# Load order and opening of a fused S5 scan and GEGLU kernel: one queue for nearly all loads, the D row spread by a product, dt computed as a row, sines ahead of the first Gelu

## The chip, the cores and the metric

The kernel runs on one core of one Trainium2 chip. The time is the device time of one execution in microseconds; the kernel before has a median of 190.36 us over three runs (189.83 to 191.79).

## The reference, cut to what matters

```python
xn = _layernorm(x)                        # x: [1, 2048, 512] bf16
# A: a diagonal complex recurrence over 2048 steps, state width P = 512
dt = jnp.exp(log_dt); Lam_bar = jnp.exp(dt * Lam)
B_bar = ((Lam_bar - 1.0) / Lam)[:, None] * Bmat
Bu = jnp.einsum("bld,pd->blp", xn + 0j, B_bar)
h = Lam_bar[None, :] * h + Bu[:, t, :]    # for t in range(L)
s = 2.0 * jnp.einsum("blp,dp->bld", hseq, Cmat).real + xn * Dskip
# B: GEGLU feed-forward, F = 1376
g = silu((gelu(xn @ w_gate) * (xn @ w_up)) @ w_down)
out = x + s * g
```

The weights w_gate and w_up are [512, 1376], w_down is [1376, 512], B and C have a real and an imaginary part of [512, 512] each. log_dt, Lambda_re, Lambda_im and Dskip are vectors of 512. Everything comes in bf16.

## The kernel before, in words

The 2048 tokens are cut into four chunks of 512 (index s), and each chunk into four tiles of 128 tokens (index m). For each chunk the kernel does five things.

- It normalises the tiles (`stats`, `rstd`, `norm_dve`; for chunks 2 and 3 `norm_act`, on ScalarE, whose sums go through the tile `junk`) and transposes them to `xnT`: chunk 0 on TensorE (`head_t`, four 128x128 transposes and an eviction by ScalarE, L341), the later chunks by DMA transposes (`dma_t`, L363).
- It multiplies `xnT` by w_gate and w_up. F is cut into thirds of 512, 512 and 352 columns. The products go into one of three PSUM slots of two banks; ScalarE evicts them to `gt` (with the Gelu) and `ub`, VectorE multiplies both to `at`, and a DMA transpose brings `at` to `atT` (L454). In chunk 0 the three thirds are done one after the other for all four tiles (`first_chunk`, then `gate_pair`, L385 to L391); in later chunks tile by tile (`gate_tile`).
- `half(s, h)` computes one half of the 512 complex states: products of `BT` and `xnT` (L530), evicted by ScalarE to `U` (L533), a rotation of `U` by tables of sines and cosines (L544, L552), a real scan with the decay `rho` (L563), and the rotation back into `hst`. This turns the complex recurrence into two real ones.
- `down_pair` multiplies `atT` by w_down and puts a Silu on it (`g2`).
- `y_tile` multiplies `hst` by the scaled C (`C2`), adds the skip term `sk` = xn times the D row, multiplies by `g2`, adds x and stores the tile.

Before that, small parameters are prepared. The three vectors log_dt, Lambda_im and Lambda_re come into a tile `pv` of 12 rows and are turned into columns by one transpose on TensorE and a copy `pf` (L622, L623). GpSimd raises e to log_dt (`dt_`) and, after VectorE's multiplication, e to dt times Lambda_re (`rho`); both are `power`, at L320. VectorE makes an angle `ang` and a folded angle `kr` for 49 table entries (L589 to L593), ScalarE takes their sines and cosines (L594, L595) and VectorE builds the full tables `tab` from them by six products and sums (L609). ScalarE's Gelu, Silu and sine lie in tables of which one is loaded at a time; a change of table is an ACT_TABLE_LOAD.

The columns of C are scaled by coefficients (`coefficients`, L672 to L690) that need `rho` and the sines; C itself comes by two DMA transposes into the second `hst` buffer (`CT`, L739). For each of four blocks ScalarE makes a product `tF` (L742) and VectorE two more (L744, L747).

The order of the work is made by a planner (`Plan`). Each step is added with its engine, a cost, a lag until others see its result, what it reads and writes, and a rank. TensorE's steps keep the order in which they are added; the steps of the other engines are put in order by a list scheduler that tries priorities with random changes and keeps the best. The costs and lags are written out by hand. Instructions of one engine run in the planned order, and an instruction that waits holds up everything behind it on that engine. DMAs issued by SP, ACT and POOL are rows of those engines' streams.

The loads of the kernel before: x tiles 0 and 2, the first two thirds of w_gate, the second chunk of x and both parts of B go through SP; x tiles 1 and 3 and the first two thirds of w_up through ACT; `pv`, the D row (copied to all 128 partitions by the DMA, L649), the last thirds of w_gate and w_up and w_down (L652, L653) through POOL. Ten matmuls on a zeroed tile `warm` (L330) fill TensorE's time until the first tile is normalised.

Of the kernel before, what the change touches and what calls it, by code (L numbers as in the profile page):

```python
# [18 lines left out]
LOOK, HOLD, TABLE, ROUNDS, TRIALS = 0.3, 8.0, 6.0, 6, 600  # L19
# [3 lines left out]
class Plan:  # L23
# [89 lines left out]
    def run(self):  # L113
# [38 lines left out]
def kernel(  # L152
# [55 lines left out]
    pv = sb("pv", [12, P])  # L208
# [25 lines left out]
    def small(name, w=NPT):  # L234
        return sb(name, [P, w], FP32)
# [30 lines left out]
    def load_w(put, eng, q, c, land, which, **kw):  # L266
        a, b = CH[c]
        nm, w, r = (("wg", wg, wg_r), ("wu", wu, wu_r))[which]
        put(eng, 0.47, land, lambda w=w, r=r: q.dma_start(out=w[:, :, a:b], in_=r[:, :, a:b]), writes=[(nm, c)], **kw)
# [5 lines left out]
    dma_first(SP, 0.5, 8.5, lambda: nc.sync.dma_start(out=x_tok[:, M : 2 * M, :], in_=x_r[:, M : 2 * M, :]), [("x", 1, m) for m in range(M)])  # L275
    for i, v in enumerate((A_log_dt, A_Lambda_im, A_Lambda_re)):
        dma(POOL, 0.6, 4.3, lambda i=i, v=v: G.dma_start(out=pv[4 * i : 4 * i + 4, :], in_=v.rearrange("(k p) -> k p", p=P)),
            writes=[("pv", i)], rank=200.0)
    ident = sb("ident", [P, P])
    pool(0.8, lambda: make_identity(nc, ident[:]), writes=["ident"], rank=190.0)  # L280

    warm = sb("warm", [P, TS])
# [5 lines left out]
    dve(480, lambda: V.memset(warm[:], 0.0), writes=["warm"], not_before=0.6, rank=300.0)  # L288
# [6 lines left out]
    acts(1, lambda: act(out=tiny[:], in_=zero[:], func=AF.Silu), ["zero"], ["tiny"], table="silu", rank=150.0)  # L295
# [17 lines left out]
    def stats(s, m):  # L313
        def f():
            V.bn_stats(out=st[:, s, m, :], in_=x_tok[:, s * M + m, :])
        dve(512, f, [("x", s, m)], [("st", s, m)])
        dve(6, lambda: V.bn_aggr(out=mv[:, s, m, :], in_=st[:, s, m, :]), [("st", s, m)], [("mv", s, m)])
# [489 lines left out]
```

## Time and profile before

| | |
|---|---|
| median of three runs | 190.36 us |
| the profiled execution | 189.71 us |
| its span, first to last instruction | 187.9 us |
| mean granted TensorE clock | 0.982 |
| TensorE, VectorE, ScalarE, GpSimd busy | 176.6, 159.2, 117.3, 15.4 us |
| first gate product | at 8.93 us |
| last product ends | at about 183.8 us |
| HBM read and written | 6.46 MB, 2.10 MB |

The span is that of one execution; 1.8 us of its time lie outside it. A row of a stage table gives, for a stretch of the span, each engine's busy time and in brackets its count of instructions (TensorE's matmuls, its weight loads, VectorE, ScalarE, GpSimd), then the granted TensorE clock as a share of full speed, the busy share of the DMA engines and what they moved. A row in order of time gives the start, the duration, the engine (SPq, ACTq and POOLq are the sequencers that issue DMAs), the line, the operation, what it writes and reads, and in square brackets how long the engine had been idle before it and what ended that.

### The profile page before, as it was taken

The page shows a single profiled execution, that of the slowest core. Times are in us where ns is not written, and L with a number is a line of the kernel's source. Part 1 is how long each engine was busy: PE and PEld are TensorE (multiplying, and loading weights), DVE is VectorE, ACT ScalarE, POOL GpSimd, SP SyncE. Part 2 cuts the span into 40 slices and gives each one's busy share as a digit, 9 for nine tenths or more (in the row PEclk, how much of TensorE's full clock was granted, in tenths as well). Part 3 has the DMA queues.
Part 4 walks back from the last instruction along what each step waited for, and adds up shares of the span by engine and source line. Part 5 has one row for each costly group of instructions (what it writes and reads, how often), then busy time and mean ns, then how long its engine had stood idle before and what let it go on. Part 6 is the DMA issues. An engine that isn't in the chain of part 4 may idle for free.

```text
span 187.9 us, 2371 instructions
## 1 busy us (share of the span) xinstructions
PE 176.6 (94%) x844; PEld 82.9 (44%) x844; DVE 159.2 (85%) x264; ACT 117.3 (62%) x172; POOL 15.4 (8%) x28
## 2 busy tenths in 40 slices
PE   7499999959999999999999999999999999899991
PEld 2144444624444445444444545544445555344440
DVE  3756699959999999999999999999999999960062
ACT  3229988589979989956438974615728656244220
POOL 7543600000000020000002000000000000000000
PEclk9859999999999999999999999999999999999999
DMA  5999389999200045580001265440110055440011
GB/s 168 288 265 272 84 229 172 240 266 214 51 0 0 0 77 105 87 153 0 0 28 58 65 130 102 77 77 3 56 56 0 0 106 97 81 115 28 0 56 56
DMA packets 45227, 18.14 MB, mean 97 GB/s; under 512 B 38496, under 2 KB 44672, under 8 KB 45216
## 3 DMA queue, kind: packets, MB, share of 16 engines
q1 hardware_dynamic: 43120, 14.42, 37.8%
q0 software_dynamic: 752, 2.26, 4.2%
q10 hardware_dynamic: 1344, 1.31, 2.0%
q8 instruction: 6, 0.10, 0.2%
q14 instruction: 5, 0.04, 0.1%
HBM read 6.46 MB, written 2.10 MB: 46 GB/s over the span
## 4 chain that ended last, share of the span: by engine, by line
DVE 62%; PE 15%; DMA 6%; issue 5%; SPq 5%; ACT 4%; DVEq 0%; ACTq 0%
DVE Fs L563 19%; DVE Q L544 16%; PE ybank L490 6%; PE slot L471 5%; PE slot L404 4%; DVE at L446 4%; DMA wg<-in_B_w_gate_dram 4%; DVE hst L556 3%; DVE yg L496 3%; SPq L363 2%; DVE W L556 2%; DMA hst<-in_A_C_im_dram 2%; SPq L739 2%; DVE ot L504 2%; DVE sk L367 2%
## 5 line engine op out<-in xcount | busy, mean ns | idle before, releaser
L428 PEld LDWEIGHTS <-xnT 128*128 128x128 bf16 x288 | 28.2, 98 | 29.2 <-issue 0.7
L471 PE MATMUL slot<-wd,atT 128*128 128x512 bf16 (+1 forms) x176 | 38.7, 379 | 0.0
L428 PE MATMUL slot<-wg,xnT 128*128 128x512 bf16 (+1 forms) x144 | 31.8, 357 | 0.5 <-ACT gt L436 0.5
L428 PE MATMUL slot<-wu,xnT 128*128 128x512 bf16 (+1 forms) x144 | 31.8, 357 | 0.0
L530 PE MATMUL slot<-xnT,BT 128*128 128x512 bf16 x128 | 28.3, 379 | 2.0 <-ACT gt L390 2.0
L490 PE MATMUL ybank<-C,hst 128*128 128x512 bf16 x128 | 29.1, 379 | 0.7 <-ACT ybank L486 0.7
L563 DVE TENSOR_TENSOR_SCAN Fs<-rho,ini,W 128x512 bf16<-128x512 f32 x24 | 29.1, 1265 | 0.0
L471 PEld LDWEIGHTS <-atT 128*128 128x128 bf16 (+1 forms) x176 | 17.2, 98 | 20.9
L533 ACT ACTIVATE U<-slot 128x1024 bf16<-128x1024 f32 x16 | 16.4, 1035 | 11.4 <-PE slot L530 11.4
L496 DVE TENSOR_TENSOR yg<-ybank,g 128x512 bf16<-128x512 f32 x14 | 9.6, 689 | 13.2 <-PE ybank L490 12.8
L530 PEld LDWEIGHTS <-BT 128*128 128x128 bf16 x128 | 12.5, 98 | 17.1 <-issue 2.2
L486 ACT ACTIVATE ybank<-sk 128x512 f32<-128x512 bf16 x14 | 8.4, 602 | 17.4 <-DVE yg L496 16.8
L490 PEld LDWEIGHTS <-hst 128*128 128x128 bf16 x128 | 12.5, 98 | 15.1 <-issue 1.0
L544 DVE TENSOR_TENSOR Q<-Fs,tab 128x4096 bf16<-128x4096 bf16 x8 | 18.3, 2291 | 0.2
L544 DVE TENSOR_TENSOR Q<-U,tab 128x4096 bf16<-128x4096 bf16 x8 | 18.3, 2286 | 0.3
L475 ACT ACTIVATE g<-slot 128x1024 f32<-128x1024 f32 x8 | 8.2, 1022 | 12.9 <-PE slot L471 12.9
L436 ACT ACTIVATE ub<-slot 128x1024 bf16<-128x1024 f32 x12 | 12.2, 1018 | 3.2 <-PE slot L428 3.2
L436 ACT ACTIVATE gt<-slot 128x1024 bf16<-128x1024 f32 x12 | 12.2, 1018 | 2.4 <-PE slot L428 2.4
L721 ACT ACTIVATE junk<-x_tok 128x512 bf16<-128x512 bf16 x16 | 10.3, 643 | 0.2
L563 DVE TENSOR_TENSOR_SCAN Fs<-rho,W 128x512 bf16<-128x512 f32 x8 | 9.3, 1208 | 0.0
L385 PEld LDWEIGHTS <-xnT 128*128 128x128 bf16 x64 | 6.3, 98 | 5.5
L320 POOL TENSOR_TENSOR rs<-sx,mhalf 128x4 f32<-128x4 f32 x2 | 2.1, 1067 | 76.1 <-DVE sx L729 43.9
(118 smaller groups left out, 197.2 us busy)
## 6 DMA issues: line engine op xcount, KB each, us to landing
out_dram<-ot SPq DMA_DIRECT2D x16, 128.0 KB, 1.7
x_tok<-in_A_x_dram SPq DMA_DIRECT2D x3, 512.0 KB, 5.5
wd<-in_B_w_down_dram POOLq DMA_DIRECT2D x1, 1280.0 KB, 10.0
wg<-in_B_w_gate_dram SPq DMA_DIRECT2D x2, 512.0 KB, 9.3
wu<-in_B_w_up_dram ACTq DMA_DIRECT2D x2, 512.0 KB, 10.5
wg<-in_B_w_gate_dram POOLq DMA_DIRECT2D x1, 352.0 KB, 4.9
wu<-in_B_w_up_dram POOLq DMA_DIRECT2D x1, 352.0 KB, 5.3
x_tok<-in_A_x_dram ACTq DMA_DIRECT2D x2, 128.0 KB, 3.1
```

Source lines behind the costliest of these rows:

```text
L428: T.matmul(ps[:, bank, 0 : b - a], lhsT=xnT[:, k, t0 : t0 + P], rhs=wt[:, k, a:b], start=(k == 0), stop=(k == KT - 1))
L436: acts(1024, lambda ps=ps, dst=dst, fn=fn: act(out=dst[:, 0:1024].rearrange("p (c w) -> p c w", c=2), in_=ps[:, :, :], func=fn), [("slot", ...
L471: T.matmul(ps[:, b, :], lhsT=atT[:fs, k, m * P : (m + 1) * P], rhs=wd[:fs, k, :], start=(k == 0), stop=(k == NFT - 1))
L486: acts(512, lambda: act(out=bank[:], in_=sk[s % 2][:, m, :], func=AF.Copy), [("sk", s % 2, m)], [("y", i)])
L490: T.matmul(bank[:, :], lhsT=hst[s % 2][:, j // NPT, j % NPT, m * P : (m + 1) * P], rhs=C2[:, j // NPT, j % NPT, :], start=(j == 0 and not ...
L496: dve(512, lambda: V.tensor_tensor(out=yg[e][:], in0=bank[:], in1=g2[gi][:, b, :], op=ALU.mult), [("y", i), ("g2", gi)], [("yg", e)])
L530: T.matmul(ps[:, ri, :], lhsT=BT[:, ri, k, pt * P : (pt + 1) * P], rhs=xnT[:, k, (s % 2) * TS : (s % 2 + 1) * TS], start=(k == 0), stop=(k ...
L533: acts(1024, lambda q=q, ps=ps: act(out=U[ui][:, :, q, :], in_=ps[:, :, :], func=AF.Copy), [("slot", i, 0), ("slot", i, 1)], [("U", ui, q)])
L544: dve(4096, lambda: V.tensor_tensor(out=Qf, in0=src.unsqueeze(1).to_broadcast(WQ), in1=table, op=ALU.mult), reads, ["Q"], rate=2.0)
L556: dve(2048, lambda: V.tensor_tensor(out=dst, in0=Qf[:, 0, :, :], in1=Qf[:, 1, ::-1, :], op=ALU.add), ["Q"], writes, rate=2.0)
L563: pl.add(DVE, 1.116 if s == 0 else 1.19, lambda ri=ri, q=q, pt=pt, first=first: V.tensor_tensor_scan(out=Fs[:, ri, q, :], data0=rho[:, pt ...
L721: acts(512, lambda i=i, fn=fn, m=m: act(out=junk[:], in_=x_tok[:, s * M + m, :], func=fn, accum_out=sx[:, s, i, m : m + 1]), [("x", s, m)] ...
```

## The change

Seven things are changed.

1. All loads but one are issued by SP, in this order: four x tiles, the first third of w_up, the second thirds of w_gate and w_up, the second chunk of x, both parts of B, the last thirds, w_down. The first third of w_gate is issued by ACT, behind the three parameter vectors, which also move there. GpSimd issues only the D row.
2. The D row is loaded into one partition. A TensorE product with a column of ones (the tile `warm`, which is now `junk` and holds ones instead of zeros) spreads it into PSUM, and ScalarE copies it to `Drow`.
3. dt is computed as a row before the transposition: ScalarE's Exp on the log_dt row, VectorE's product with Lambda_im (`pr`). Four small products, two of them in fp32 with the identity `id4`, turn Lambda_im, Lambda_re, dt and dt times Lambda_im into columns. These steps (`parameters`) stand between the fillers and the first transposes instead of after the first gate product. ScalarE loads the table of Exp, and then that of the sine, before the first eviction.
4. The first Gelu is planned after both sines (`early`).
5. In chunk 1 the `y_tile` steps come one gate tile later (`late`).
6. Costs and lags in the plan are changed at several places, C's transposes among them.
7. The planner tries 1200 instead of 600 random changes, half of them begun in the first 20 us of its own time.

The diff, cut to its core:

```diff
-LOOK, HOLD, TABLE, ROUNDS, TRIALS = 0.3, 8.0, 6.0, 6, 600
+LOOK, HOLD, TABLE, ROUNDS, TRIALS = 0.3, 8.0, 6.0, 6, 1200
...
-                lo = rng.uniform(-10.0, 170.0)
+                lo = rng.uniform(-10.0, rng.choice((20.0, 170.0)))
...
-    for m, (eng, q, land) in enumerate(((SP, nc.sync, 1.9), (ACT, nc.scalar, 2.1), (SP, nc.sync, 2.1), (ACT, nc.scalar, 2.4))):
-        dma_first(eng, 0.47, land, lambda m=m, q=q: q.dma_start(out=x_tok[:, m, :], in_=x_r[:, m, :]), [("x", 0, m)], not_before=0.72)
-    for c, which, eng, q, land in ((0, 0, SP, nc.sync, 3.5), (0, 1, ACT, nc.scalar, 5.0), (1, 0, SP, nc.sync, 6.0), (1, 1, ACT, nc.scalar, 7.5)):
-        load_w(dma_first, eng, q, c, land, which)
...
     for i, v in enumerate((A_log_dt, A_Lambda_im, A_Lambda_re)):
-        dma(POOL, 0.6, 4.3, lambda i=i, v=v: G.dma_start(out=pv[4 * i : 4 * i + 4, :], in_=v.rearrange("(k p) -> k p", p=P)),
-            writes=[("pv", i)], rank=200.0)
+        dma_first(ACT, 0.45, 2.5, lambda i=i, v=v: nc.scalar.dma_start(out=pv[i][:], in_=v.rearrange("(k p) -> k p", p=P)),
+            [("pv", i)], not_before=0.72)
+    for m in range(M):
+        dma_first(SP, 0.45, 1.75 + 0.12 * m, lambda m=m: nc.sync.dma_start(out=x_tok[:, m, :], in_=x_r[:, m, :]), [("x", 0, m)], not_before=0.72)
+    load_w(dma_first, ACT, nc.scalar, 0, (0.47, 3.9), 0)
+    for c, which, land in ((0, 1, 3.3), (1, 0, 3.1), (1, 1, 2.9)):
+        load_w(dma_first, SP, nc.sync, c, (1.45, land), which)
...
+    for which in range(2):
+        load_w(dma_first, SP, nc.sync, 2, (1.0, 2.7), which)
...
+    dma(POOL, 0.7, 2.2, lambda: G.dma_start(out=Drow[0:1, :], in_=A_Dskip.rearrange("(a d) -> a d", a=1)), writes=["Drow"], rank=200.0)
+    pool(0.25, lambda: G.tensor_copy(out=id4[:], in_=ident[0:4, 0:4]), ["ident"], ["id4"], rank=190.0)
...
-    acts(1, lambda: act(out=tiny[:], in_=zero[:], func=AF.Silu), ["zero"], ["tiny"], table="silu", rank=150.0)
+    acts(1, lambda: act(out=tiny[:], in_=zero[:], func=AF.Exp), ["zero"], ["tiny"], table="exp", rank=150.0, after=[first[ACT]])
+    acts(128, lambda: act(out=pr[0][:], in_=pv[0][:], func=AF.Exp), [("pv", 0), "tiny"], ["dtr"], table="exp", rank=150.0)
+    acts(1, lambda: act(out=tiny[:], in_=zero[:], func=AF.Sin), ["zero", "dtr"], ["tiny"], table="silu", rank=150.0)
+    dve(128, lambda: V.tensor_tensor(out=pr[1][:], in0=pv[1][:], in1=pr[0][:], op=ALU.mult), [("pv", 1), "dtr"], ["thr"], base=0.13, rank=150.0)
...
-                kw = {"table": "gelu"} if nm == "wg" else {}
+                kw = {"table": "gelu", "after": early} if nm == "wg" else {}
...
-        pt_ps = slots[2][:, 0, :].bitcast(BF16)[:, 0:12]
-        pe(1, 60, lambda: T.transpose(pt_ps, pv[:, :], ident[0:12, 0:12]), [("pv", i) for i in range(3)] + ["ident"], [("slot", 2, 0)])
-        dve(12, lambda: V.tensor_copy(out=pf[:], in_=pt_ps), [("slot", 2, 0)], ["pf"], rank=10.0)
-        power(dt_[:], e_t[:], ldt, 4, ["pf", "e_t"], ["dt"])
-        dve(4, lambda: V.tensor_tensor(out=thn[:], in0=lim, in1=dt_[:], op=ALU.mult), ["pf", "dt"], ["thn"])
...
+        def f():
+            for i, (src, idn) in enumerate(((pv[1], ident[0:4, 0:4]), (pv[2], ident[0:4, 0:4]), (pr[0], id4[:]), (pr[1], id4[:]))):
+                T.matmul(pt_ps[:, 4 * i : 4 * i + 4], lhsT=src[:], rhs=idn, start=(i == 0), stop=(i == 3))
+        pe(4, 150, f, [("pv", 1), ("pv", 2), "dtr", "thr", "ident", "id4"], [("slot", 2, 0)])
+        pe(1, 512, lambda: T.matmul(slots[2][:, 1, :], lhsT=warm[0:1, 0:P], rhs=Drow[0:1, :], start=True, stop=True), ["Drow", "warm"], [("slot", 2, 1)])
+        acts(512, lambda: act(out=Drow[:], in_=slots[2][:, 1, :], func=AF.Copy), [("slot", 2, 0), ("slot", 2, 1)], ["Drow"], rank=50.0)
+        dve(16, lambda: V.tensor_copy(out=pf[:], in_=pt_ps), [("slot", 2, 0), ("slot", 2, 1)], ["pf", "thn", "dt"], rank=10.0)
...
-    dummies(10, 0)
+    dummies(8, 0)
+    parameters()
+    dummies(2, 0)
...
-    dma(POOL, 1.0, 3.0, lambda: G.dma_start(out=Drow[:], in_=A_Dskip.partition_broadcast(P)), writes=["Drow"], rank=-20.0)
-    for which in range(2):
-        load_w(dma, POOL, G, 2, 6.0, which, not_before=10.0)
-    dma(POOL, 1.0, 8.0, lambda: G.dma_start(out=wd[:, 0 : NFT - 1, :], in_=B_w_down[0 : (NFT - 1) * P, :].rearrange("(k p) d -> p k d", p=P)), writes=["wd"], not_before=19.0)
+    dma_first(SP, 3.6, 2.7, lambda: nc.sync.dma_start(out=wd[:, 0 : NFT - 1, :], in_=B_w_down[0 : (NFT - 1) * P, :].rearrange("(k p) d -> p k d", p=P)), ["wd"])
...
-        dma(SP, 1.4, 4.0, lambda ri=ri, src=src: nc.sync.dma_start_transpose(out=CT[:, ri, :, :], in_=src),
+        dma(SP, 2.4, 2.7, lambda ri=ri, src=src: nc.sync.dma_start_transpose(out=CT[:, ri, :, :], in_=src),
             writes=[("CT", ri)], after=[turned[1]])
...
+            late = 2 if s == 1 else 1
+            if not last and m >= late:
+                y_tile(s - 1, m - late)
+                skip(s + 1, m - late)
```

Most of the order is the planner's, so three places are shown as the engines' instruction streams. Line numbers behind L272 are higher by 1 to 13 in the changed kernel.

The first place is VectorE while chunk 0 is normalised, from the second tile's statistics on; the words in brackets name whose semaphore an instruction waits for (DMAHW with a number is the completion of one load). Before:

```order
L315 BN_STATS st<-x_tok 128x6 [waits DMAHW0_49]
L317 BN_AGGR mv<-st 128x2 [waits DVE_49]
L323 TENSOR_SCALAR ve<-mv 128x1 [waits DVE_49]
L357 TENSOR_SCALAR xn_90<-x_tok,mv,rs 128x512 [waits Pool_49]
L315 BN_STATS st<-x_tok 128x6 [waits DMAHW3_49]
L357 TENSOR_SCALAR xn_91<-x_tok,mv,rs 128x512 [waits Pool_49]
```

Now:

```order
L327 BN_STATS st<-x_tok 128x6 [waits DMAHW3_49]
L307 TENSOR_TENSOR pr_74<-pv_71,pr_73 4x128 [waits DMAHW2_49,Activation_49]
L335 TENSOR_SCALAR ve<-mv 128x1 [waits DVE_49]
L329 BN_AGGR mv<-st 128x2 [waits DVE_49]
L335 TENSOR_SCALAR ve<-mv 128x1 [waits DVE_49]
L327 BN_STATS st<-x_tok 128x6 [waits DMAHW5_49]
L638 COPY pf<-slot_111 128x16 [waits Activation_49]
L369 TENSOR_SCALAR xn_94<-x_tok,mv,rs 128x512 [waits Pool_49]
```

The product `pr` and the copy `pf` have come in ahead of the first normalised tile (xn_90 before, xn_94 now), and `pf` waits for ScalarE's copy of the spread D row, the fourth ScalarE instruction.

The second place is ScalarE at the last third of chunk 0, around the first product with C. Before:

```order
L389 ACTIVATE ub_81<-slot_105 128x352
L390 ACTIVATE gt_79<-slot_105 128x352
L742 ACTIVATE tF<-hst_73,cim 128x1024
L389 ACTIVATE ub_81<-slot_106 128x352
L390 ACTIVATE gt_79<-slot_106 128x352
```

Now:

```order
L401 ACTIVATE ub_86<-slot_109 128x352
L402 ACTIVATE gt_84<-slot_109 128x352
L732 ACTIVATE junk,sx<-x_tok 128x512
L545 ACTIVATE U_89<-slot_110 128x2x512
L732 ACTIVATE junk,sx<-x_tok 128x512
L545 ACTIVATE U_89<-slot_111 128x2x512
L732 ACTIVATE junk,sx<-x_tok 128x512
L545 ACTIVATE U_87<-slot_109 128x2x512
L753 ACTIVATE tF<-hst_77,cim 128x1024
```

`tF` stood between the evictions of the first and the second of four tiles; now it follows the evictions of all four and three of the second chunk's U evictions, and the first of them follows a sum over the third chunk of x.

The third place is the stream of DMAs on SP from the second chunk of x to the third one. Before:

```order
L275 DMA x_tok<-in_A_x_dram 128x4x512
L582 DMA_TRANSPOSE BT<-in_A_B_re_dram 128x4x512
L582 DMA_TRANSPOSE BT<-in_A_B_im_dram 128x4x512
L363 DMA_TRANSPOSE xnT<-xn_91 128x4x128
L363 DMA_TRANSPOSE xnT<-xn_93 128x4x128
L363 DMA_TRANSPOSE xnT<-xn_90 128x4x128
L363 DMA_TRANSPOSE xnT<-xn_92 128x4x128
L739 DMA_TRANSPOSE hst_73<-in_A_C_re_dram 128x4x512
L739 DMA_TRANSPOSE hst_73<-in_A_C_im_dram 128x4x512
L717 DMA x_tok<-in_A_x_dram 128x4x512 x2
```

Now:

```order
L282 DMA_TRANSPOSE BT<-in_A_B_im_dram 128x4x512
L270 DMA wg<-in_B_w_gate_dram 128x4x352
L270 DMA wu<-in_B_w_up_dram 128x4x352
L663 DMA wd<-in_B_w_down_dram 128x10x512
L375 DMA_TRANSPOSE xnT<-xn_97 128x4x128
L375 DMA_TRANSPOSE xnT<-xn_95 128x4x128
L375 DMA_TRANSPOSE xnT<-xn_94 128x4x128
L375 DMA_TRANSPOSE xnT<-xn_96 128x4x128
L664 DMA wd<-in_B_w_down_dram 96x512
L750 DMA_TRANSPOSE hst_77<-in_A_C_re_dram 128x4x512
L750 DMA_TRANSPOSE hst_77<-in_A_C_im_dram 128x4x512
L728 DMA x_tok<-in_A_x_dram 128x4x512 x2
```

The last thirds and w_down, which POOL issued beside this stream, now stand in it, ahead of the second chunk's transposes and of C.

More of the change, by code (lines that the diff above doesn't have):

```diff
@@ L207 @@
     C2 = sb("C2", [P, 2, NPT, D])
-    pv = sb("pv", [12, P])
+    pv = [sb(f"pv{i}", [4, P]) for i in range(3)]
+    pr = [sb(f"pr{i}", [4, P], FP32) for i in range(2)]
     Drow = sb("Drow", [P, D])
@@ L637 @@
     head_t(0)
[L638 removed]
+    dummies(1, 1)
     head_t(1)
@@ L760 @@
             at_t(s, m, 0, 2)
-            if not last and m > 0:
-                y_tile(s - 1, m - 1)
-                skip(s + 1, m - 1)
+            late = 2 if s == 1 else 1
+            if not last and m >= late:
+                y_tile(s - 1, m - late)
+                skip(s + 1, m - late)
         if not last:
-            y_tile(s - 1, M - 1)
-            skip(s + 1, M - 1)
+            for m in range(M - late, M):
+                y_tile(s - 1, m)
+                skip(s + 1, m)
             for h in range(2):
```

54 lines of the change are left out of this document (27 added, 27 removed).

## The prediction

> **What bounds the kernel now.** I read the page's busy shares first, then the same by stage, then who waits for whom on TensorE, then the lines in order of time at the two places where TensorE stands still.
>
> ```profile
> span 187.9 us, 2371 instructions
> PE 176.6 (94%) x844; PEld 82.9 (44%) x844; DVE 159.2 (85%) x264; ACT 117.3 (62%) x172; POOL 15.4 (8%) x28
> ```
>
> The chain of waits runs mostly through VectorE, which is nearly as full, but beside it TensorE works almost without a gap. By stage (each engine's busy us, then granted clock, DMA share, GB/s):
>
> ```profile
> 4.50:7.90 3.40, 1.71 (x12) 0.66 (x11) 3.25 (x11) 1.08 (x2) 2.27 (x4) 1.00 0.99 294
> 7.90:11.40 3.50, 2.47 (x10) 1.13 (x10) 1.06 (x5) 0.25 (x2) 0.65 (x1) 0.51 1.06 305
> 11.40:14.80 3.40, 3.40 (x12) 1.47 (x12) 2.95 (x11) 1.61 (x3) 2.66 (x3) 0.50 1.20 181
> 14.80:18.20 3.40, 3.40 (x18) 1.51 (x17) 2.64 (x5) 3.14 (x4) 1.03 (x1) 1.00 1.13 327
> 18.20:37.80 19.60, 19.60 (x102) 9.87 (x101) 17.37 (x44) 15.68 (x23) 3.43 (x5) 1.00 0.95 181
> 37.80:40.00 2.20, 0.21 (x3) 0.01 (x1) 0.10 (x2) 1.92 (x4) 0.00 (x0) 1.00 0.99 288
> 40.00:61.20 21.20, 21.20 (x100) 9.77 (x100) 21.03 (x26) 19.92 (x34) 0.00 (x0) 1.00 0.44 88
> 61.70:163.00 101.30, 101.30 (x496) 48.44 (x496) 100.01 (x137) 64.80 (x94) 2.13 (x2) 1.00 0.30 61
> 163.80:183.90 20.10, 20.01 (x92) 8.83 (x91) 7.08 (x15) 6.34 (x8) 0.00 (x0) 1.00 0.19 53
> 183.90:187.90 4.00, 0.00 (x0) 0.00 (x0) 1.06 (x2) 0.00 (x0) 0.00 (x0) 1.00 0.19 66
> ```
>
> From 14.8 on, TensorE (first busy column) is busy all the time at full clock, but for 37.8 to 40.0 and two short gaps. So the end is: the moment of the first gate product, plus what the half clock costs until 14.8, plus a fixed amount of products, plus the gaps, plus a tail of 4.0 us. The change touches neither the products nor the tail. The gaps, from the waits of TensorE:
>
> ```profile
> PE slot L530 <- ACT gt L390: 2.0, 1, 2.0
> PE slot L404 <- DMA wg<-in_B_w_gate_dram: 1.6, 1, 1.6
> PE ybank L490 <- ACT ybank L486: 0.7, 1, 0.7
> PE slot L428 <- ACT gt L436: 0.5, 1, 0.5
> ```
>
> **Part 1, the gap at 38 us.**
>
> ```profile
> 29.88 3.68 SPq L739 DMA_TRANSPOSE hst<-in_A_C_re_dram  x1
> 33.60 2.35 SPq L739 DMA_TRANSPOSE hst<-in_A_C_im_dram  x1
> 38.09 1.15 ACT L742 ACTIVATE tF<-hst,cim 128x1024 f32<-128x1024 bf16 x1 [2.75 <-DMA hst<-in_A_C_im_dram]
> 39.14 0.45 ACT L389 ACTIVATE ub<-slot 128x352 bf16<-128x352 f32 x1
> 39.99 7.07 PE L530 MATMUL slot<-xnT,BT 128*128 128x512 bf16 x32 [1.99 <-ACT gt L390]
> ```
>
> ScalarE reaches the first product with C (tF) before C_im has landed, stands 2.75 us, and the evictions queued behind it keep all three PSUM slots full. In the changed order tF stands behind the last third's evictions and three of the next U evictions, so none of those waits for C. What ScalarE meets instead is the first statistics line (junk), which waits for the third chunk of x (x2 below). TensorE gets to the second half's products about 3 us earlier than 39.99, at 37, and can fill three slots (three quarters of the 7.07, 5.2 us) before it needs the eviction behind junk. So x2 must land by about 40. C lands in the quiet order of one queue; what stands ahead of it is Part 3. I take the whole 2.0 off. Bounds: 2.0 gained, nothing gained.
>
> **Part 2, the start.** The first chunk's stretch in the chain of waits, rows of the first 9 us, and the landing times of the three small parameter loads (min/median/max):
>
> ```profile
> 1.64 7.25 DMA wg<-in_B_w_gate_dram
> 1.26 0.72 POOL L277 DMA_DIRECT2D pv<-in_A_Lambda_re_dram  x1 [0.83 <-POOLq L791]
> 1.65 1.07 ACTq L269 DMA_DIRECT2D wu<-in_B_w_up_dram  x2
> 2.75 1.28 ACT L295 ACT_TABLE_LOAD   x1 [2.75 <-issue]
> 4.04 0.20 ACT L295 ACTIVATE tiny<-zero 128x1 f32<-128x1 f32 x1
> 3.57 0.69 DVE L315 BATCH_NORM_STATS2 st<-x_tok 128x6 f32<-128x512 bf16 x1 [2.26 <-DMA x_tok<-in_A_x_dram]
> 5.60 0.41 DVE L357 TENSOR_SCALAR xn<-x_tok,mv,rs 128x512 bf16<-128x512 bf16 x1
> 6.50 0.60 ACT L341 ACTIVATE xnT<-ybank 128x512 bf16<-128x512 bf16 x1 [2.26 <-PE ybank L338]
> 8.93 1.87 PE L404 MATMUL slot<-wg,xnT 128*128 128x512 bf16 x4 [1.55 <-DMA wg<-in_B_w_gate_dram]
> DMA to landing us min/median/max: 3.3/5.2/5.7
> ```
>
> Before, the operand was ready at 7.10 and the first chunk of w_gate came at 8.93. It was issued third on SP, beside ACT's queue; up to it both queues carried two x tiles and one weight chunk each, 1.5 MB. Now ACT's queue holds only it and 3 KB, and SP's holds x and then w_up: with equal turns it lands after 1.05 to 1.3 MB, an estimate of 5 to 6.2 of the former 7.25 us, so at 7.1 to 8.3.
>
> The operand becomes later. VectorE runs pf, and behind it xn, after ScalarE's copy of the spread D row. Upper branch: ACT issues four loads (about 0.5 each, as the pair at 1.65), a table load 1.28, tiny 0.2, Exp 0.3 (guessed from the 0.2), the second table load 1.28, tiny: free at 5.9. Lower branch: VectorE multiplies theta after the second statistics, 5.4; TensorE's four small products to about 5.7; the D product, one 512-wide matmul at half clock, 0.6, to 6.3. The D row itself is POOL's first load, like the one at 1.26, and that kind landed after 3.3 us, at 4.6. Then in line: copy 0.6, pf 0.16, xn 0.41, four transposes 0.4, eviction 0.60, and five hops of 0.04: 8.7. So the operand now sets the start, and the gain shrinks from the 1.8 that stood between operand and weight to 0.2. Bounds: if pf held nothing, operand at 7.1 and w_gate at 7.4, 1.5 gained; if the D row takes 5.7 us as the slowest of the three small loads, it lands at 7.0, the chain ends at 10.0, 1.1 lost. I take 0.2 gained, nearest to the first of the three loads, whose place the D row has.
>
> The half clock. It was granted from 7.9 to 14.8, though the 3.4 us before 7.9 had 1.71 us of products and the first 3.5 us after it 2.47; only 3.40 of 3.40 brought 1.00 back. In the new order transposes, filler and gate products follow each other from 7.6 on, where before 8.93 ended a gap of 1.55: the continuous stretch begins 1.3 us earlier, 0.2 of which is counted. A half clock that ends 1.1 us earlier is worth 0.5 us. Bounds: a whole stretch of 3.4 us at full instead of half clock either way, 1.7. I take 0.5 gained. [...]
>
> **Part 3, the loads in one queue.** The six loads of w_up, of the last thirds and of w_down join SP: by ACT's pair and POOL's rows some 0.5 to 1.1 us of issue each, 4 to 5 us on SP, which nobody waits for as long as the data queue ahead is longer. It is:
>
> ```profile
> 20.00:25.00 5.00, 5.00 (x25) 2.25 (x23) 3.63 (x21) 4.96 (x10) 3.43 (x5) 1.00 0.29 56
> 25.00:30.00 5.00, 5.00 (x25) 2.25 (x23) 4.97 (x12) 3.66 (x9) 0.00 (x0) 1.00 1.38 266
> 22.23 1.13 POOL L652 DMA_DIRECT2D wd<-in_B_w_down_dram  x1
> L363 SPq DMA_TRANSPOSE xnT<-xn x4: 1189/1676/2585, 22.5 to 27.8; - x4
> wd<-in_B_w_down_dram POOLq DMA_DIRECT2D x1, 1280.0 KB, 10.0
> x_tok<-in_A_x_dram SPq DMA_DIRECT2D x3, 512.0 KB, 5.5
> ```
>
> The DMA engines idle from 20 to 25 (share 0.29) and are full from 25 on, because w_down was issued at 22.2 and ran beside the transposes of the second chunk and C. Now w_down follows the last thirds directly, about 20 to 25 at the 266 GB/s of the full stretch (1.31 MB, 4.9 us), and x2 is through some 4 us earlier: by 39. That keeps Part 1's condition with 1 us to spare. Cost: nothing, hidden by TensorE's 19.60 busy of 19.60; without that cover, up to the rival's price below. [...]
>
> **Part 4, sines before the Gelu, and the rest.**
>
> ```profile
> 18.77 1.28 ACT L594 ACT_TABLE_LOAD   x1
> 34.12 2.29 DVE L544 TENSOR_TENSOR Q<-U,tab 128x4096 bf16<-128x4096 bf16 x1
> 26.42 1.22 DVE L609 TENSOR_TENSOR Q<-cp,ch 128x2048 bf16<-128x2048 bf16 x1
> ```
>
> Two table loads of 1.28 leave the stretch of 18.8 to 23.5 and one joins the start (counted). TensorE did not wait there, so they are worth nothing directly. The six 1.22 us table products on VectorE began at 26.42 because their operands came late; now they fill gaps from about 18 on, and the scan's first rotation can start near 30 instead of 34.12. VectorE thereby gains some 4 us of lead, which covers its added copies (0.2 each). If that cover were gone VectorE, 21.03 of 21.20 us busy, would set the pace. The lead is what may shorten the gaps of 0.5 and 0.7, of which the second ends with VectorE's output. The order after 60 is new as well and may hold gaps of its own. I take 0.4 off the 1.2. Bounds: 1.2 gained, 1.5 lost (two gaps of the former kinds more).
>
> **Sum.** 0.2 + 0.5 + 2.0 + 0.4 = 3.1 us. The profiled execution took 189.71 us (span 187.9 and 1.8 around it): 186.6. The median of the runs shown is 190.36, 0.65 above it, and the comparison is with that: 187.3.
>
> **The rivals.**
> A, the gain is eaten. The start comes at 10.0 (1.1 lost, by the slow small load) and half the gap at 38 returns as a wait for x2: 1.0 + 0.4 + 0.5 - 1.1 = 0.8 gained, 189.6. For it: landings of 5.2 and 5.7. Against: the load's place is the first. Chance 0.21.
> B, slower: w_down ahead of the transposes in one queue. If it takes 10.0 us again, from 22 to 32, the four transposes behind it (four times 1.676, 6.7 us) end at 38.7, C (3.68 and 2.35) at 44.7, x2 some 3 us later at 48; ScalarE stands at junk until then, and the eviction that frees the fourth slot comes about 2 us after, at 49.9; the stage that ended at 46.9 ends at 51.6, 4.7 lost; less the 0.4 of the later gaps, 194.7. It decides from x2 landing later than about 43.5. Against it: the 10.0 were measured beside the very transposes that now wait. Chance 0.08.
> C, the clock stays up. Filler and small products raise the 1.71 of 3.40 enough that no half clock is granted at all, or one stretch less (1.7 instead of 0.5), and the start comes at 7.9 (1.0 instead of 0.2): 5.1 gained, 185.3. Chance 0.11.
> D, that the change does nothing: the order is visibly other at each place, so only its effect can fail; it is in A.
>
> **How the numbers follow.** The forecast has 0.60: 185.7 to 188.9 on its own, the clock term moving it most. With A inside and C inside, the range is 185.0 to 189.8; above lies B and part of A. A measurement of this kernel tells about 1% (1.9 us) from no change, that is 188.46. Faster: C and nine tenths and more of the forecast, 0.68; within 1%: A and the rest, 0.24; slower: B, 0.08.
>
> **What would show it.** Right: no TensorE wait over 0.5 us between 15 and 160; first gate product near 8.7 released by ScalarE's eviction and not by w_gate; pf on VectorE ended by ScalarE; w_down landed before 26; the U rotation starting near 30. Wrong: ScalarE waiting for x_tok near 38 (B), a first gate product past 9.5 with the D product waiting for its row (A), or VectorE waits for DMA in the first 20 us. If TensorE is gapless and the time is still above 188.5, the bound was misread.

## The result, and the profile after

The changed kernel takes 183.56 us (median of four runs, 183.30 to 184.22) beside 190.10 us (188.50 to 191.79) for the kernel before on the same chip: ratio 0.969, 95% interval 0.962 to 0.976. Twelve more executions in later comparisons gave 183.32 to 185.83; the median of all sixteen is 183.99. A ratio leaves out executions more than 1.5% above the fastest of the same kernel, so where the kernel before lost little clock a few times, its common 190.3 is partly left out, and medians are given beside the ratios. It is faster, and by more than the prediction's whole range (185.0 to 189.8): 6.8 us below the 190.36 that the prediction started from, where 3.1 was forecast.

The first lines of the page after, and its stages (busy us of TensorE, its weight loads, VectorE, ScalarE, GpSimd, then granted clock, DMA share, GB/s):

```profile
span 182.4 us, 2385 instructions
PE 176.1 (97%) x850; PEld 83.2 (46%) x850; DVE 158.4 (87%) x264; ACT 118.3 (65%) x174; POOL 11.0 (6%) x21
```

```profile
4.50:7.90 3.40, 3.15 (x13) 1.23 (x12) 1.62 (x9) 1.68 (x3) 1.11 (x2) 1.00 1.06 353
7.90:11.40 3.50, 3.50 (x23) 2.02 (x24) 3.36 (x13) 1.96 (x4) 1.20 (x2) 1.00 1.08 374
11.40:14.80 3.40, 3.40 (x21) 1.55 (x19) 2.90 (x8) 3.31 (x7) 1.32 (x2) 1.00 1.23 222
18.20:37.80 19.60, 19.60 (x102) 9.89 (x101) 19.11 (x30) 15.79 (x26) 1.13 (x1) 1.00 1.13 250
37.80:61.20 23.40, 23.40 (x115) 11.03 (x113) 23.23 (x50) 22.80 (x36) 0.00 (x0) 1.00 0.26 48
61.20:163.00 101.80, 101.66 (x497) 48.45 (x496) 98.33 (x133) 62.58 (x91) 2.11 (x2) 1.00 0.35 67
```

TensorE's waits, all of them:

```profile
PE slot L342 <- DVE junk L297: 1.6, 1, 1.6
PE slot L416 <- ACT gt L421: 0.3, 1, 0.3
PE ybank L350 <- DVE xn L369: 0.3, 1, 0.3
```

The gap at 38 us is gone, the two later gaps are gone, and the granted clock shows no half clock between 7.9 and 14.8. Rows of the opening and of the stretch around 38 us:

```profile
6.52 1.03 PE L342 MATMUL slot<-junk 128*128 128x512 bf16 x2
9.11 1.27 PE L416 MATMUL slot<-wg,xnT 128*128 128x512 bf16 x4
10.43 1.03 PE L416 MATMUL slot<-wg,xnT 128*128 128x512 bf16 x4
15.39 1.89 PE L416 MATMUL slot<-wu,xnT 128*128 128x512 bf16 x8 [0.26 <-ACT gt L421]
28.58 2.35 SPq L750 DMA_TRANSPOSE hst<-in_A_C_im_dram  x1
28.73 2.29 DVE L556 TENSOR_TENSOR Q<-U,tab 128x4096 bf16<-128x4096 bf16 x1
35.70 7.07 PE L542 MATMUL slot<-xnT,BT 128*128 128x512 bf16 x32
42.00 1.14 ACT L753 ACTIVATE tF<-hst,cim 128x1024 f32<-128x1024 bf16 x1
```

The products of the second half (the 32 with `BT`) are a good checkpoint: nothing but the opening and the gap at 38 lies ahead of them. They start at 35.70 instead of 39.99, 4.3 us earlier. The gap was 2.0 of that, so the opening gave 2.3. Spans fell by 5.5 (187.9 to 182.4); the other 1.2 is the two later gaps (0.7 and 0.5). The rest of the 6.8 is where the profiled executions lie to their medians: 189.71 was 0.65 below the one, 184.22 is 0.66 above the other.

The opening's 2.3 did not come from an earlier start. The first gate product is 0.2 later than before (9.11 and 8.93), and a new wait of 0.26 stands at 15.39. So what went of the half clock was worth some 2.8.

It did not all go. In these traces the granted clock stands at 1.00 before its first loss whatever the rate, so the rate has to be read from the durations, and they show that this execution began at half rate: products of 512 columns start 0.43 us apart up to 9.5 and 0.22 us apart from 9.8 on. Four of them take 1.87 us at half rate (at 8.93 in the kernel before) and 1.03 at the full one (at 10.43 here). In the kernel before the full rate came at about 4.6, was lost at 7.9 and came back at 14.8. Here it came for the first time at about 9.6 and stayed. Half rate ended 5.2 us earlier, which at half of that is an estimate of 2.6, close to the 2.8.

### The profile page after: what moved, and what is told of

It is laid out like the page before. It is cut to its first block, busy times and chain, and to the rows that moved or that the text cites. A ratio compares the mean times of both kernels' runs of the same rounds, so it can differ in the third digit from the quotient of the medians.

```text
span 182.4 us, 2385 instructions
## 1 busy us (share of the span) xinstructions
PE 176.1 (97%) x850; PEld 83.2 (46%) x850; DVE 158.4 (87%) x264; ACT 118.3 (65%) x174; POOL 11.0 (6%) x21
## 4 chain that ended last, share of the span: by engine, by line
PE 55%; DVE 35%; ACT 5%; issue 3%; DVEq 0%
PE slot L440 18%; PE ybank L502 11%; PE slot L483 10%; DVE Fs L575 10%; DVE Q L556 9%; PE slot L542 6%; PE slot L397 4%; PE slot L342 2%; PE slot L416 2%; DVE C L758 1%; DVE at L458 1%; DVE hst L564 1%; DVE hst L568 1%; DVE C L755 1%; DVE sk L379 1%
## 5 line engine op out<-in xcount | busy, mean ns | idle before, releaser
L458 DVE TENSOR_TENSOR at<-gt,ub 128x1024 bf16<-128x1024 bf16 x12 | 8.1, 676 | 0.0
```

What stands on the lines that cost most here:

```text
L458: dve(1024, lambda: V.tensor_tensor(out=at[j][:, 0:1024], in0=gt[q][:, 0:1024], in1=ub[q][:, 0:1024], op=ALU.mult), qs[0] + qs[1], [("at", ...
```

## The experiments

All are timed beside the kernel before on the same chip, in five rounds. Its own executions scatter with the granted clock, which weighs in every ratio. All 49 of them in these comparisons (one of 378.21 us is left out), against the 16 of the changed kernel. A stretch is here 3.4 us at half clock: the kernel before lost two, one behind the other, in its profile (0.51 and 0.50 in the rows from 7.9 to 14.8), the changed kernel one in its second profile (0.53 in the row from 7.9 to 11.4, 0.98 in the next). One lowers the mean clock of 189 us by 0.009, two by 0.018, and for an execution without a trace the number lost is estimated from that:

```
mean granted clock   before: executions, median us   changed: executions
0.968 to 0.971        6   192.07                      0
0.976 to 0.982       25   190.31                      0
0.986 to 0.991        9   189.14                      3
0.994 to 1.000        9   188.00                     13
```

The kernel before is 2.3 us faster when no lost stretch is recorded (190.31 and 188.00), and that is so in 9 of 49 executions; 31 lost two stretches or more by their mean clock. The mean clock is a rough measure: a half rate before the first rise isn't in it (the changed kernel's, up to 9.5, stood under 1.00), and a loss at the end is in it, where TensorE has little left to do (in the second profile of the changed kernel the row from 178.3 to 182.4 has a clock of 0.97, and TensorE was busy for 0.44 of its 4.10 us).

**Filler in the kernel before.** Theory K: the clock term was mis-sized, and it is decided by how full TensorE is just ahead of the first gate products.

```diff
-            for _ in range(k):
+            for _ in range({10: 12}.get(k, k)):
...
                 T.transpose(tp[:, k, :], src[:, k * P : (k + 1) * P], ident[:])
+            for _ in range(3 if n == 1 else 0):
+                T.matmul(slots[2][:, 0, :], lhsT=warm[:, 0:P], rhs=warm[:], start=True, stop=True)
```

> The kernel before with five more matmuls on the zeroed tile: two more ahead of the first transposes and three between the second tile's transposes and the first gate product, where TensorE stood still for 1.55 us waiting for w_gate. The order of everything else is that of before. Theory K (the gain that I missed is the clock: before, the half clock came back ahead of the first gate product and lasted 6.8 us; with the stretch filled it lasts at most half of that): granted clock 0.99 or more, full clock by about 11.4, and 1.5 to 2.9 us less than before. [...]

Median 188.41 of five (before 190.14), 1.7 less, ratio 0.989 (0.983 to 0.995); executions at 186.40, 186.65 and 188.41 had a clock of 1.00, those at 189.01 and 190.61 had 0.991. One of 660.90 is left out. Why 188.41 is 2.0 above 186.40 at the same recorded clock isn't known; only 186.40 has a trace. The opening of its profile:

```profile
4.50:7.90 3.40, 2.59 (x17) 1.11 (x16) 3.24 (x11) 1.08 (x2) 2.23 (x4) 1.00 0.95 271
7.90:11.40 3.50, 2.35 (x14) 0.99 (x12) 1.20 (x5) 0.71 (x2) 0.65 (x1) 1.00 1.02 284
```

The row from 4.5 holds 2.59 us of products instead of 1.71, and the row that had 0.51 has 1.00, though TensorE is no busier in it than before (2.35, 2.47). K holds: three of five executions show no lost stretch and two show one, where the kernel before mostly loses two. In this profile the gap at 38 shrank as well, to 0.9, with C_im issued at 29.99 instead of 33.60, so 1.1 of this execution's gain is not the clock's.

**The changed kernel without filler.**

```diff
-            for _ in range(k):
+            for _ in range(0 * k):
```

> The changed kernel without any of the eleven filler matmuls; TensorE's first work is the small parameter products at about 5.1. Nothing of the result hangs on the fillers. Theory K: continuous work begins at 7.8 only, so full clock comes between 11 and 14.6 instead of about 9.4: 1 to 2.5 us more than the changed kernel's 183.6, so 184.6 to 186. [...]

Median 185.13 (184.06 to 185.18), 1.6 above the changed kernel's 183.56 and 1.1 above the median of its sixteen executions; the changed kernel was not timed in this group, and the ratio to the kernel before, 0.973 (0.970 to 0.976), lies among its own (0.969 to 0.976). The profile is clearer: the first gate product starts 0.9 earlier than with filler, half rate lasts until some 13 instead of 9.6, and the second half's products start at 36.68, 1.0 later:

```profile
8.21 1.89 PE L416 MATMUL slot<-wg,xnT 128*128 128x512 bf16 x4 [0.26 <-ACT xnT L353]
12.45 2.19 PE L416 MATMUL slot<-wg,xnT 128*128 128x512 bf16 x8
```

Four products in 1.89 us against eight in 2.19 show the change of rate. K holds, with the price near its lower end.

**The kernel before with only the first tF moved**, behind seven evictions of U on ScalarE:

```diff
+        move(nth(ACT, ("tF",), 0), [i for i in order if self.tags[i][0] == ACT and self.tags[i][1] and self.tags[i][1][0][0] == "U"][6])
```

(`tags` remembers each step's engine and what it writes, `nth` finds a step, `move` puts it behind another in the finished order.)

> The kernel before with one step moved in ScalarE's order alone: the first product tF with C stands behind seven of eight U evictions of the first two chunks instead of between the last third's evictions, as in the changed kernel. Loads and all else as before. My step in the prediction: TensorE's gap of 2.0 us at 38 goes, 2.0 us less, 188.1 (at 190.1 for before). Rival M (the gap was the late DMA chain, and what is behind it comes late too): the wait moves on to the transposes of the second chunk or to the sums over x, and less than 0.7 us is gained.

Median 187.27 (185.88 to 188.73), ratio 0.983 (0.979 to 0.988). The gap is gone although C still comes late: C_im was issued at 35.39 in its profile, later than the 33.60 of before, and the second half's products start without a wait.

```profile
35.39 2.14 SPq L750 DMA_TRANSPOSE hst<-in_A_C_im_dram  x1
38.71 7.07 PE L541 MATMUL slot<-xnT,BT 128*128 128x512 bf16 x32
```

So the order on ScalarE is enough. The 2.9 between the medians is more than 2.0 by the scatter of the clock, which the groups of the table take out: the two executions at 1.00 (185.88 and 186.33) lie 1.9 below the 188.00 of before, the three at 0.986 to 0.991 (median 187.29) 1.9 below 189.14, and the profiled one at 0.979 (188.73) 1.6 below 190.31. The price of 2.0 was about right.

**Both in the kernel before**, filler and tF:

> The kernel before with the fillers of the first experiment (two more at the start, three behind the second tile's transposes) and the first tF moved behind seven U evictions. If the clock (about 2 us measured for the fillers) and the gap at 38 us (2.0 us in the trace) are two separate terms, the sum is 4 to 5 us less than before: 185.1 to 186.1, and what is left to the changed kernel's 183.56 is the later gaps (0.9) and the rest. If they are one (the gap only shows with the slow start), 187 to 188.5.

Median 185.70 (185.37 to 186.87), all six at a clock of 0.998 or more. The time lies in the range expected of two separate terms, but it is 3.6 and not 4 to 5 below its neighbour's 189.30, and the ratio, 0.986 (0.981 to 0.991), is no lower than that of tF alone: in this group the kernel before lost little clock in three of eleven executions. By the groups of the table the two add up: 190.31 with two stretches lost, 188.00 with none, 185.70 with tF moved as well; filler makes the second step the rule. Its profile is the bridge from the one kernel to the other:

```profile
PE slot L417 <- DMA wg<-in_B_w_gate_dram: 1.4, 1, 1.4
PE slot L441 <- ACT gt L449: 0.7, 1, 0.7
PE ybank L503 <- ACT ybank L499: 0.7, 1, 0.7
```

```profile
9.46 1.02 PE L417 MATMUL slot<-wg,xnT 128*128 128x512 bf16 x4 [1.42 <-DMA wg<-in_B_w_gate_dram]
35.61 7.07 PE L543 MATMUL slot<-xnT,BT 128*128 128x512 bf16 x32
```

Its first gate product comes at 9.46, still behind w_gate's late landing, and yet it stands at the checkpoint at 35.61, level with the changed kernel's 35.70. So between these two executions the clock and tF alone explain everything up to 36 us; the loads, the sines and the D row bring nothing there that filler does not. Spans then differ by 1.4 (183.8 and 182.4), which are the two later gaps that it still has, 0.7 each.

**The kernel before without filler.**

```diff
-            for _ in range(k):
+            for _ in range(0 * k):
```

> The kernel before without any filler products. Theory K (the early full clock there was lost again in the window from 4.5 to 7.9, which was half empty, so that the fillers bought nothing): the gate products start at 8.93 as before and run cold until some 13.5 to 14.8, as they run at half clock until 14.78 before: 189.5 to 190.5, no change. Rival F (fillers help whatever comes after them): 191.5 to 193.

Median 191.50 (189.63 to 193.26) beside 189.30, ratio 1.013 (1.007 to 1.020): slower, so K's 189.5 to 190.5 fails as a number, and the time lies in rival F's range. In the one profile the loss is not in the opening, which runs at half rate until some 15 (four products in 1.87 us at 9.30), as the kernel before did until 14.8:

```profile
39.50 1.15 ACT L742 ACTIVATE tF<-hst,cim 128x1024 f32<-128x1024 bf16 x1 [3.74 <-DMA hst<-in_A_C_im_dram]
41.40 8.75 PE L530 MATMUL slot<-xnT,BT 128*128 128x512 bf16 x32 [2.98 <-ACT gt L390]
41.00:44.40 3.40, 3.00 (x10) 1.19 (x10) 3.02 (x5) 3.40 (x6) 0.00 (x0) 0.73 1.17 156
44.40:47.80 3.40, 3.40 (x13) 1.39 (x12) 3.37 (x4) 2.75 (x6) 0.00 (x0) 0.77 1.19 241
```

C came 1.4 us later in that execution, the gap grew from 2.0 to 3.0, and this time a stretch of half clock followed it (0.73 and 0.77 in the two rows): 32 products took 8.75 us instead of 7.07. So in this execution the wait was followed by 1.7 us more, where the gap of 2.0 in the kernel before was followed by none. Five of the six executions had a mean clock of 0.988 to 0.991, so one lost stretch is common here; that it is the same one in each, and that C's lateness comes from the missing filler, isn't shown.

**The last thirds and w_down issued by GpSimd again**, all else as changed:

```diff
-        load_w(dma_first, SP, nc.sync, 2, (1.0, 2.7), which)
+        load_w(dma_first, SP, G, 2, (1.0, 2.7), which)
...
-    dma_first(SP, 3.6, 2.7, lambda: nc.sync.dma_start(out=wd[:, 0 : NFT - 1, :], in_=B_w_down[0 : (NFT - 1) * P, :].rearrange("(k p) d -> p k d", p=P)), ["wd"])
+    dma_first(SP, 3.6, 2.7, lambda: G.dma_start(out=wd[:, 0 : NFT - 1, :], in_=B_w_down[0 : (NFT - 1) * P, :].rearrange("(k p) d -> p k d", p=P)), ["wd"])
...
```

> The changed kernel with the last thirds of both weights and w_down issued by GpSimd again, at the same places of the planned order; all else unchanged. My step in the prediction: the loads have a lead that TensorE's gapless work hides, so within 0.7 us of the changed kernel, 183.3 to 184.3. Rival N (one queue in order of need is what made the gain): w_down runs beside the transposes and C again, ScalarE or TensorE wait near 37, and 1.5 us or more is lost, 185 or more.

Median 184.24 (183.30 to 185.59), inside the changed kernel's own scatter; TensorE's waits are the same three rows, and the checkpoint is at 35.84. GpSimd issued w_down at 17.97, SP at 16.36 in the changed kernel, so both were early. Which queue these loads use is worth nothing that can be measured; that they are issued before 20 us is common to both.

**The start, three ways.** The changed kernel's first gate product hangs on pf, which waits 1.74 us for ScalarE's copy of the D row; these rows of the changed kernel show it:

```profile
6.63 0.60 ACT L637 ACTIVATE Drow<-slot 128x512 bf16<-128x512 f32 x1 [1.03 <-PE slot L636]
7.26 0.17 DVE L638 COPY pf<-slot 128x16 f32<-128x16 f32 x1 [1.74 <-ACT Drow L637]
8.45 0.60 ACT L353 ACTIVATE xnT<-ybank 128x512 bf16<-128x512 bf16 x1 [1.23 <-PE ybank L350]
```

The first way takes the D row out of that line and three fillers with it:

```diff
+        t1 = nth(PE, ("y", 1), 0)
+        move(nth(PE, ("slot", 2, 1), 0), t1)
+        move(nth(ACT, "Drow", 0), nth(ACT, ("xnT", 0, 1), 0))
+        move(nth(DVE, "pf", 0), nth(DVE, "ang", 0), False)
...
-            for _ in range(k):
+            for _ in range({2: 0, 1: 0}.get(k, k)):
```

> The changed kernel, with the D row's product moved on TensorE behind the second tile's transposes, ScalarE's eviction of it behind the second tile's, VectorE's copy of pf behind the third xn, and the three fillers after the parameters' products taken away. In the changed kernel's profile the first gate product stands at 9.11 and its operand hangs on pf, which VectorE holds 1.74 us for ScalarE's Drow eviction; w_gate's first chunk lands at 6.65. Theory P (the D row's detour sets the start): first transposes near 6.2, first gate product at 7.2 to 7.6, 1.5 to 1.9 us earlier; matmuls ran cold until about 9.35 there, so that a part of the earlier work runs at half rate, which gives back 0.7 to 0.9: 182.4 to 183.0 against 183.56. Rival Q (something else holds the start, w_gate's landing or the norms): first gate product at 8.5 or later, 183.3 to 183.8. [...]

The second moves pf alone:

```diff
+        move(nth(DVE, "pf", 0), nth(DVE, "ang", 0), False)
```

> The changed kernel with only VectorE's copy of pf moved behind the third xn; fillers and the D row's product stay ahead of the first transposes on TensorE. Theory P: xn for the first two tiles is ready near 6.3 and no longer waits for ScalarE; TensorE's own order (two fillers to 7.55) then decides: first transposes at 7.55 instead of 7.81, 0.25 us less, 183.2 to 183.5. Rival Q: nothing, 183.5 to 183.8. These two differ by less than the interval, so the place of the transposes in the profile decides.

Medians 183.73 and 183.56, ratios 0.973 and 0.974 beside the 0.969 to 0.976 of the changed kernel, which was not timed in this group: no gain that can be measured. The first way's first gate product came where it was expected, the second way's transposes earlier (6.07, not 7.55); the worth was not there. One of the first way's six executions took 189.17 at a mean clock of 0.947; it has no trace. First gate products and checkpoint of the first way, then of the second:

```profile
7.58 1.89 PE L430 MATMUL slot<-wg,xnT 128*128 128x512 bf16 x4
9.68 1.28 PE L430 MATMUL slot<-wg,xnT 128*128 128x512 bf16 x4
35.21 7.07 PE L556 MATMUL slot<-xnT,BT 128*128 128x512 bf16 x32
```

```profile
7.89 1.02 PE L427 MATMUL slot<-wg,xnT 128*128 128x512 bf16 x4 [0.99 <-DMA wg<-in_B_w_gate_dram]
34.24 7.07 PE L553 MATMUL slot<-xnT,BT 128*128 128x512 bf16 x32
```

The first way starts 1.53 earlier and runs its first four products in 1.89 us, at half rate, so that only 0.5 is left at the checkpoint. The second had the full clock in its profiled execution and was 1.46 ahead at the checkpoint; two new waits for ScalarE later on (0.4 and 0.3) left 0.8 of it in the span. In the changed kernel itself the same happens from one execution to the next. In its second profile the clock was up early (two fillers took 0.60 us instead of 1.03), so that the first gate product came at 8.10, and was then lost for one stretch, until 11.5:

```profile
5.73 0.60 PE L342 MATMUL slot<-junk 128*128 128x512 bf16 x2
8.10 1.89 PE L416 MATMUL slot<-wg,xnT 128*128 128x512 bf16 x4 [0.25 <-ACT xnT L353]
7.90:11.40 3.50, 3.30 (x11) 1.46 (x12) 3.36 (x13) 1.55 (x5) 0.81 (x3) 0.53 1.09 376
36.13 7.07 PE L542 MATMUL slot<-xnT,BT 128*128 128x512 bf16 x31
```

It came to the checkpoint at 36.13, 0.4 behind the execution that started 1.0 later.

> The changed kernel once more, unedited, beside the next one on the same chip: 183.3 to 184.3.

It measured 183.89 (183.32 to 185.83). A third profile, of the changed kernel beside the last version below, is of the first kind: first gate product at 9.11, full rate from about 9.8, second half's products at 35.81.

The third way issued w_gate's first chunk ahead of the parameter rows on ScalarE's queue:

```diff
+        move(nth(DVE, "pf", 0), nth(DVE, "ang", 0), False)
+        move(nth(ACT, ("wg", 0), 0), nth(ACT, ("pv", 0), 0), False)
```

> The changed kernel with pf moved behind the third xn, as before, and w_gate's first chunk issued on ScalarE's queue ahead of the three parameter rows instead of behind them (1.2 us earlier by the issue rows). Theory P (an earlier first gate product is worth its time as long as the clock is full there): with pf out of the way the first gate product waited for w_gate at 7.89; with w_gate 0.8 to 1.2 earlier it stands at 7.0 to 7.3, and the whole comes to 1.0 to 1.8 less than the changed kernel run beside it. Rival T (what is won ahead of 9 us is given back, at half rate while the clock has not come up, or in waits for ScalarE's Gelu at 15): first gate product at 7.0 to 7.3 all the same, and the time within 0.5 of the changed kernel's.

Both theories were wrong: median 188.87 of eleven (one of 482.99 is left out) beside the changed kernel's 183.89, 5.0 us slower.

```profile
1.90 0.25 ACTq L285 DMA_DIRECT2D pv<-in_A_Lambda_im_dram  x1
5.09 0.26 ACTq L285 DMA_DIRECT2D pv<-in_A_Lambda_re_dram  x1
9.06 0.18 PE L646 MATMUL slot<-ident,pv 4*128 4x4 bf16 x1 [3.14 <-DMA pv<-in_A_Lambda_re_dram]
12.66 1.89 PE L428 MATMUL slot<-wg,xnT 128*128 128x512 bf16 x4
```

The 1 KB rows now stood behind 512 KB, the third one's issue was held until 5.09, and TensorE waited for it until 9.06 with the first transposes queued behind. The first gate product came at 12.66, 3.6 later than in the changed kernel, and at half rate. The order on this small queue moves more than any other single edit here, because the parameters stand ahead of the transposes in TensorE's order.

**Early and full.** The last version adds three fillers behind the second tile's transposes to the second way (the edit of the first experiment, in slot 1, beside the move of pf).

> The changed kernel with pf moved behind the third xn and three more fillers behind the second tile's transposes, where TensorE stood 0.99 us for w_gate. Theory P: first gate product at 7.6 to 8.0 and no half clock after it in any execution, so that the second half's products start at 34.2 to 34.6 instead of 35.7; 0.4 to 1.0 less than the changed kernel beside it (the first trial gave back 0.66 of 1.46 in later waits), and mean clocks of 0.994 or more throughout. Rival T (the order behind 36 us gives it all back): within 0.3 of the changed kernel.

> The changed kernel unedited, beside the next one on the same chip: 183.3 to 184.3.

Median 183.62 (183.03 to 185.12) beside 184.54 (183.38 to 184.89) for the changed kernel on that chip, with clocks of 1.00 in five of six executions. Its ratio to the kernel before is 0.972 (0.966 to 0.977), the changed kernel's 0.974 (0.968 to 0.979): the intervals overlap, so the 0.9 is as forecast and not established.

```profile
7.32 1.03 PE L429 MATMUL slot<-wg,xnT 128*128 128x512 bf16 x4
34.22 7.07 PE L555 MATMUL slot<-xnT,BT 128*128 128x512 bf16 x31
PE ybank L515 <- ACT ybank L511: 0.5, 1, 0.5
PE slot L555 <- ACT gt L415: 0.4, 1, 0.4
```

The opening is 1.5 us better and the span 0.5 (181.9): waits for ScalarE (the two shown) take most of the rest back, here too.

## Why the prediction was right and wrong

- **The gap at 38 us** (2.0): right in place, size and mechanism. The move of tF alone removes it, for 1.9 at equal mean clock. That w_down be out of C's way was not needed for this: with C issued at 35.39 there is no gap either, and with w_down on GpSimd's queue the time is the same.
- **The half clock** (0.5): this is the step that failed. Two rows had shown the half clock, and the prediction kept both stretches and let them end 1.1 us earlier, as if they moved with the start of the continuous work. In the profile after, half rate ended 5.2 us earlier, at 9.6, and no loss followed; in the second profile one stretch was lost instead of two, and it ended at 11.5. What the sum left out, and had only in its bounds as one stretch of 1.7, is that the number of lost stretches changes, here with the filler ahead of and around the first gate products (2.59 us of products instead of 1.71 in the row from 4.5 to 7.9). By the mean clock two stretches or more were lost in 31 of 49 executions of the kernel before, in none of eleven with filler there, and in none of the sixteen of the changed kernel. The term was worth 2.8 between the profiles (2.3 net of a start 0.2 later and the new wait), and 2.3 by the scatter of the kernel before. The 3.15 of 3.40 us that TensorE was busy ahead of 7.9, instead of 1.71, don't measure this by themselves: they are products at half rate, 0.43 us apart and not 0.22. Rival C had named a change of their number, at 0.11, and priced it at 1.7 as one stretch less, when the profile showed two; its start at 7.9 did not come. That the two prices of 2.3 agree so well is partly luck, as the mean clock leaves out half rate before the first rise (1.00 up to 9.5 in the profile after).
- **The start** (0.2 gained): the chain was right, operand through the D row and not w_gate, and pf ended by ScalarE, but 0.2 was lost and not gained: the first gate product came at 9.11, 0.4 after the 8.7, as TensorE's small products, fillers and transposes ahead of it ran at half rate (two fillers in 1.03 us); 8.10 in the execution where they did not (0.60). The size mattered little, since much of what an earlier start won was lost again: 1.53 us became 0.5 at half rate in the first way, and 1.46 became 0.8 through ScalarE's later waits in the second.
- **The later gaps** (0.4 of 1.2): all of the 1.2 was gained. The rotation of U at 28.73 instead of 34.12 is the lead that the prediction named; that this lead is the cause was argued, not tried. The later place of `y_tile` in chunk 1 and the longer search of the planner are untried rivals, and the timing alone moves these waits: of 0.7 and 0.5 only 0.5 is left in the kernel before without filler, whose order is that of before.
- **Part 3 and rivals A and B**: nothing of A or B came; no wait for x2 shows. The last thirds and w_down in SP's queue were neither a gain nor a cost that could be measured.

So 2.0 + 2.3 + 1.2 = 5.5 between the profiles, in place of 2.0 + 0.7 + 0.4.

What stays open is what keeps the clock. The busy time ahead of 7.9 orders the executions only roughly: in the row from 4.5 to 7.9, 1.71 of 3.40 us lost it, and 2.38 (both edits), 2.41 (pf alone) and 2.59 (filler) kept it, and yet the changed kernel's second execution lost it for one stretch behind 2.67 of 3.40:

```profile
4.50:7.90 3.40, 2.67 (x20) 1.25 (x18) 2.43 (x11) 2.12 (x4) 1.52 (x3) 1.00 1.05 355
```

No run here separates the busy time from the rest that differs between these executions, such as the products with four columns.

## What to carry to other kernels

Before costing an opening that stands between the full and the half clock, run the kernel several times and set time against mean clock: the difference of the groups is a first price of the clock term, and it can be had without any edit. Then read the durations of the first products, because a half rate that stands from the start wasn't in the mean clock here (in the changed kernel up to 9.5, under 1.00). Here filling TensorE up to its first real product was worth more (1.7 us in the kernel before) than starting that product sooner (at most 0.8 in a span, nothing clear in a median), and one product that waited for a small load queued behind a large one undid most of the gain. On ScalarE, an instruction that waits for a late DMA belongs behind the evictions on which TensorE depends; with the loads unchanged that was worth 1.9 us.

## What was new about the hardware

- The clock was lost without a long pause: in the kernel before TensorE's waits between 5 and 9 us were 0.86, 0.30 and 1.55 us with 1.71 us of products in the 3.40 from 4.5 to 7.9, the clock was lost at 7.9, some 0.5 us into the third, and two stretches at half clock followed (0.51 and 0.50, until 14.8). The longest wait there was 1.55 us, and the wait of 1.99 us at 38 in the same profile was followed by products at the full clock (32 in 7.07 us).
- A granted clock of 1.00 at the start didn't say that products ran at full rate. In the two kinds of executions above four 512-column products took 1.89 us (first way) and 1.02 us (second way), both in stretches whose recorded clock was 1.00; the kernel before without filler ran at half rate until some 15 us under the same 1.00 (four products in 1.87 us at 9.30).
- The same program, edited in nothing, had its clock up at different times: the first gate product ran at 9.11 in one execution and at 8.10 in another, because the work ahead of it ran at half rate in the one and at the full rate in the other: the small products took 0.99 and 0.58 us, the D row's product 0.58 and 0.37, two fillers 1.03 and 0.60, together 1.05 us more, and the two starts are 1.01 apart.
